# Two channel blocks of v in one load, with a newly planned instruction order, in an interleaved state-space kernel

## The chip, the cores and the metric

The kernel runs on one core of a Trainium2 chip. The metric is the device time of one execution in microseconds (us): the median of three runs. The core has five engines that run their own instruction streams and wait for each other through semaphores: TensorE (PE, matrix products, which land in eight PSUM banks), VectorE (DVE), ScalarE (ACT), GpSimd (POOL) and SyncE (SP). Transfers between the memory of the chip and the core's SBUF are started by an engine's queue, here nearly all by SP's, and are carried by 16 DMA engines.

## The reference

Four layers follow each other on a sequence of 2048 tokens with 640 channels, each added to its input: A, B, A, B, where the two A layers share their weights, and so do the two B layers.

```
x = A_x
x = x + A(layernorm(x))     # A: complex diagonal recurrence
x = x + B(layernorm(x))     # B: long convolution of k*v, gated
x = x + A(layernorm(x))
x = x + B(layernorm(x))

A(x): Lam_bar = exp(dt*Lam);  Bu = x @ B_bar.T
      h[t] = Lam_bar*h[t-1] + Bu[t]
      y = 2*Re(h @ Cmat.T) + x*Dskip
B(q): k_shift[t] = sum over l<4 of k[t-l]*shift_k[:,l]
      kv = k_shift * v
      y = causal convolution of kv with ssm_k (length 2048) + kv*ssm_D
      return q*y
```

In B only q is the layer's input; k and v are inputs of the kernel. So the long convolution y is the same in both B layers and is computed once.

## The kernel before

**Tiling.** The convolution goes in five passes, one for each block of 128 channels (yq0 to yq4), as a Fourier transform of 4096 points made of matrix products. The layers go in four chunks of 512 tokens (c0 to c3): A1c0 is the first A layer's chunk 0, B1c0 the first B layer's, A2 and B2 the second ones.

**Tasks.** The program is cut into some 900 tasks, each a few instructions with a name. The names that are needed here:

- `warm`: 18 products that warm TensorE up. `a_...`: the A layer's weights, as `a_b0` (products) with `a_b0e` (copies out of PSUM), and `a_ct` (products), `a_wc` (ScalarE) and `a_wm` (VectorE, line 493).
- `yt_...`: the tables of the transform; `yt_ph`, `yt_f2`, `yt_neg` run on VectorE, `yt_sin` on ScalarE, `yt_Ci` and `yt_Si` are DMA transposes (line 1047).
- `kv_kd`, `kv_k0`: a load of ssm_D and its cast on VectorE (line 1164).
- `kv_lk`, `kv_lv`: the load of one block of k (a DMA transpose, line 1209) and of v (line 1198). `kv_mm0:1` is the shift convolution of block 0, half 1, on TensorE; `kv_ev0:1` multiplies it by v on VectorE (line 1243). The two halves of a block are transposed by `yq0_vl` (line 1329).
- In a pass: `KA`, `KB` transform the filter, `VA`, `VB` the product kv, `pw` multiplies the two on VectorE (lines 1350 to 1354), `IB`, `tt` (DMA transpose), `IA` transform back, `st` stores the result. `yq1_IB:m3` is a group of products, `yq1_IB:e3` its copy out of PSUM (line 290 on ScalarE, 292 on VectorE).
- In an A chunk: `ln_bn`, `ln_sd`, `ln_post`, `id` normalise; `tu` transposes; `bq`, `bp` multiply by B; `eq`, `ev` copy out; `ri`, `sc`, `ro`, `hx` are the recurrence on VectorE (lines 803, 804, 820, 875); `cp` multiplies by C on TensorE (line 901), `xe` adds the result to x (line 911 on VectorE, 909 on ScalarE).
- In a B chunk: `ln_sq` and others normalise, `u`, `mm`, `m` gate and add (lines 959, 980, 982; 944 and 948 at the very end), `st` stores the output.

**Order.** No scheduler runs when the program is built: `ORDER` (line 59) is a written list of all task names, and each engine gets its instructions in that order. A letter after a name chooses the engine (`/a` ScalarE, `/d` VectorE, `/p` GpSimd). `PLACE` (line 144) gives each buffer its place in one SBUF arena (in units of 64 bytes) and each PSUM tile its first bank. Buffers share places, and an instruction waits until the last reader of what lay there before is done; so order, engines and places together set every wait. SP, too, works through its transfers in this order: one that waits holds up all behind it.

SP's transfers up to the first half of the convolution are, in this order: B_im, B_re, filter 0, k0, v0, x0, filter 1, k1, v1, `yq0_vl`, C_re, x2, C_im, filter 2, `yt_Ci`, k2, `yt_Si`, v2, x1, `yq1_vl`, k3, v3, `yq2_vl`, `yq0_tt`, x3, `A1c0_tu`, `yq3_vl`, k4, filter 3, v4, `yq0_st`. A load of v brings 2048 rows of 256 bytes (128 channels in bf16).

Of the kernel before, what the change touches and what calls it, by code (L numbers as in the profile page):

```python
# [17 lines left out]
P = 128  # L18
# [3 lines left out]
NJ = D // P  # L22
# [17 lines left out]
VN = 1  # L40
# [19 lines left out]
a_ldB1 a_ldB0 yt_io8 yt_ph8 kv_dsl kv_kd yq0_kl a_pl a_ti yt_h0 yt_io0 kv_pd2/p yt_f0 kv_lk0 kv_k0 yt_ph0 yt_f2 kv_d0  # L60
kv_lv0 warm kv_k1 a_b01:2 yt_sin8 xl0 yq1_kl kv_lk1 a_p0 kv_lv1 yt_sin0 yt_f3 a_b0e1:2/a a_p1 a_b00:4 a_b00:2 yt_neg8
kv_pd4/d kv_k2 yt_f4 kv_pd0/p a_p2 yq0_ka a_b0e0:4/a a_b01:3 yq0_KA:m0 a_b0e0:2/a a_p3 a_b00:3 a_b0e1:3/d yq0_KA:e0/d
kv_pd3/d kv_d1 kv_d2 a_p4a a_p4 kv_ds0 kv_ds1 a_dd yt_h1 kv_ds4 kv_ds3 kv_ds2 a_b00:1 a_b0e0:3/a a_b0e0:1/a a_b01:0
yt_neg0 a_b0e1:0/a a_b00:0 a_b0e0:0/a yq0_KA:m3 yq0_KA:e3/a yq0_KA:m2 kv_mm0:1 yq0_KA:e2/d kv_pd1/d a_ta yq0_KA:m1
a_b01:4 yq0_KA:e1/a kv_mm0:0 a_b0e1:4/a kv_ev0:1 a_t0 kv_ev0:0 yq0_vl a_ldC0 xl2 a_ldC1 a_p5a a_p5b yq0_KB:m0
yq0_KB:e0/a yq0_KB:m2 yq2_kl yt_Ci kv_lk2 yq0_KB:e2/a yt_Si a_p6 kv_lv2 yq1_ka a_f A1c0_ln_bn:1/d a_lamd/d yq1_KA:m1
yq1_KA:e1/a xl1 yq1_KA:m2 yq0_KB:m3 yq1_KA:m3 kv_mm1:0 yq1_KA:e3/a a_b01:1 yq1_KA:e2/a yq0_KB:e3/a kv_ev1:0 yt_h2
a_b0e1:1/a yt_h3/p a_t1 kv_mm1:1 kv_ev1:1 a_b11:3 yq0_VA:m2 a_b1e1:3/d yq0_VA:e2/d a_b11:0 a_b1e1:0/d a_b10:1
a_b1e0:1/d yq0_KB:m1 a_b11:1 a_b1e1:1/a yq0_KB:e1/d a_b11:4 yq0_VA:m1 yq0_VA:e1/a a_b1e1:4/d yq0_VA:m3 yq0_VA:m0
yq0_VA:e3/d yq1_KA:m0 yq0_VA:e0/a a_b10:4 a_t2 A1c0_ln_bn:2/d A1c0_ln_bn:3/d A1c0_ln_bn:0/d yq1_KA:e0/a a_b1e0:4/a  # L70
yq0_VB:m0 yq0_VB:e0/a a_ct1 yq0_VB:m3 a_wc01:0 a_wm01:0 yq0_VB:m2 yq0_VB:e3/a yq0_VB:e2/a a_wc01:1 A1c0_ln_sd a_b10:2
a_lm2 yq2_ka a_b1e0:2/d a_wm01:1 yq0_VB:m1 yt_nci yq1_KB:m1 yq0_VB:e1/a a_b11:2 yq1_KB:m2 yq1_KB:e1/a kv_mm2:0
a_b1e1:2/a yq1_KB:e2/a A1c0_ln_post yq0_pw:0 a_b10:3 a_b10:0 a_b1e0:3/a yq1_vl kv_mm2:1 a_b1e0:0/a kv_lk3 kv_lv3
A1c0_id:2/a A1c0_id:0/a yq1_KB:m3 yq1_KB:e3/a yq1_KB:m0 kv_ev2:1 yq1_KB:e0/a yq2_KA:m3 yq2_KA:e3/a yt_nsi kv_ev2:0
yq2_vl A1c2_ln_bn:1/d A1c2_ln_bn:3/d A1c2_ln_bn:2/d A1c1_ln_bn:2/d A1c1_ln_bn:3/d A1c2_ln_bn:0/d A1c0_id:1/a
A1c0_id:3/a A1c1_ln_bn:1/d yq0_IB:m0 yq2_KA:m0 yq0_IB:e0/a yq2_KA:e0/a yq0_IB:m1 yq0_IB:m3 yq0_IB:e1/a yq0_IB:e3/a
yq1_VA:m2 yq1_VA:m1 yq1_VA:e2/a yq0_IB:m2 A1c2_ln_sd yq1_VA:m3 yq0_IB:e2/a yq0_tt yq1_VA:m0 A1c1_ln_bn:0/d yq1_VA:e0/d
yq1_VA:e3/a yq1_VA:e1/a kv_mm3:1 a_ct4 A1c1_ln_sd yq1_VB:m1 a_wc04:0 kv_ev3:1 kv_mm3:0 A1c2_ln_post a_wm04:0
A1c1_ln_post yq1_VB:e1/a a_wc04:1 kv_ev3:0 yq1_VB:m0 A1c2_id:0/a a_wm04:1 yq1_VB:m3 a_ct0 A1c2_id:2/d A1c2_id:3/d
yq1_VB:e3/d A1c2_id:1/d xl3 A1c0_tu yq1_VB:e0/a a_wc00:0 yq1_VB:m2 yq0_IA:m1 yq1_VB:e2/a yq0_IA:m0 yq3_vl kv_lk4  # L80
yq3_kl kv_lv4 a_wm00:0 a_wc00:1 a_wm00:1 yq0_IA:e1/a yq0_IA:e0/a yq2_VA:m2 yq2_VA:e2/a yq1_pw:0 yq2_VA:m1 yq2_VA:e1/a
yq2_KA:m1 yq2_VA:m3 yq2_VA:e3/a yq2_KA:m2 a_ct2 yq2_KA:e2/a yq2_KA:e1/a a_wc02:0 yq2_VA:m0 yq2_KB:m0 yq2_VA:e0/a
yq2_KB:e0/a a_wm02:0 A1c1_id:1/d A1c1_id:0/d A1c3_ln_bn:0/d a_wc02:1 yq2_KB:m1 yq1_IB:m0 a_wm02:1 yq0_st
A1c3_ln_bn:3/d A1c3_ln_bn:1/d A1c3_ln_bn:2/d yq2_KB:e1/a yq1_IB:m3 yq1_IB:e0/a yq1_IB:e3/a a_ct3 a_wc03:0 a_wm03:0
yq1_IB:m1 yq1_IB:e1/a yq1_IB:m2 yq1_IB:e2/d a_wc03:1 a_wm03:1 yq3_ka yq2_KB:m2 A1c1_id:2/a yq2_KB:e2/a A1c3_ln_sd
yq1_tt kv_mm4:1 yq2_KB:m3 kv_ev4:1 A1c1_id:3/a yq2_KB:e3/a yq3_KA:m3 yq3_KA:m0 yq3_KA:e0/a yq3_KA:e3/d yq4_kl
yq2_VB:m0 yq2_VB:m3 yq2_VB:m2 yq2_VB:e0/d yq2_VB:e3/d yq3_KA:m2 A1c0_bq:2 A1c3_ln_post yq2_VB:e2/d yq3_KA:e2/a
kv_mm4:0 yq3_KA:m1 A1c0_eq:2/a yq2_VB:m1 A1c0_bp:2 yq3_KA:e1/a kv_ev4:0 A1c1_tu yq2_VB:e1/d yq2_pw:0 yq1_IA:m1
yq3_VA:m0 A1c0_ev:2/a yq3_VA:e0/a yq1_IA:e1/a A1c0_bq:1 A1c0_eq:1/a yq3_VA:m2 yq3_KB:m0 yq3_VA:m1 A1c0_bp:1 A1c2_tu
yq3_KB:e0/a yq3_VA:e2/a yq3_VA:e1/a yq3_VA:m3 yq3_KB:m3 yq3_VA:e3/d yq4_ka A1c3_id:1/d A1c3_id:3/d yq3_KB:e3/d  # L90
A1c3_id:0/d A1c0_ev:1/a yq2_IB:m2 yq3_KB:m2 yq2_IB:m0 yq2_IB:e2/a yq3_KB:e2/a yq3_VB:m3 yq2_IB:e0/d yq3_VB:e3/a
yq1_IA:m0 yq1_IA:e0/d A1c3_id:2/a yq3_VB:m0 yq3_VB:m2 yq3_VB:e2/d yq2_IB:m1 yq4_KA:m2 yq3_VB:e0/a a_rq yq3_KB:m1
yq3_KB:e1/a yq2_IB:m3 yq2_IB:e1/d yq2_IB:e3/a yq3_VB:m1 yq1_st A1c3_tu yq3_VB:e1/d yq3_pw:0 yq2_tt yq4_vl A1c0_bq:0
yq4_KA:e2/a A1c0_eq:0/a yq4_KA:m3 A1c1_bq:0 yq4_KA:m0 yq4_KA:e3/a yq4_KA:m1 A1c0_bp:0 yq4_KA:e0/a yq4_KA:e1/a
A1c2_bq:2 yq4_KB:m1 A1c0_ev:0/a A1c0_ri yq3_IB:m3 a_rq2 A1c0_sc A1c0_cy A1c0_ro A1c0_hx A1c1_eq:0/a yq4_KB:e1/a
A1c1_bq:2 yq2_IA:m0 A1c2_eq:2/a yq3_IB:e3/a A1c2_bp:2 yq2_IA:m1 yq2_IA:e0/a A1c2_ev:2/a A1c1_eq:2/a yq2_IA:e1/a
A1c1_xr A1c0_xr yq2_st A1c1_bq:1 yq4_KB:m2 A1c1_bp:2 A1c1_eq:1/a A1c1_bp:1 yq4_KB:e2/a A1c1_ev:2/a yq4_VA:m2 yq3_IB:m0
yq4_VA:e2/a A1c1_bp:0 yq3_IB:e0/a A1c1_ev:1/a yq4_KB:m3 A1c1_ev:0/a yq3_IB:m1 yq4_VA:m3 yq4_KB:m0 yq4_KB:e3/a
yq4_VA:e3/d yq4_KB:e0/d yq3_IB:e1/a A1c2_bq:0 A1c1_ri A1c1_sc A1c1_cy yq4_VA:m0 yq4_VA:m1 yq4_VA:e1/a A1c2_eq:0/a
A1c2_bq:1 yq3_IB:m2 yq4_VA:e0/a yq3_IB:e2/a A1c2_eq:1/a A1c2_bp:0 A1c2_ev:0/a yq4_VB:m3 yq4_VB:m2 A1c2_bp:1 yq4_VB:m0  # L100
yq4_VB:e2/a A1c2_ev:1/a yq4_VB:m1 yq4_VB:e3/a yq4_VB:e1/a A1c0_cp:1 A1c0_xe:1/a yq4_VB:e0/d yq4_pw:0 a_w10:2 yq3_tt
a_w10:1 a_w11:4 a_w1e0:2/a a_w11:0 A1c0_cp:3 a_w1e0:1/a a_w1e1:0/a a_w1e1:4/a a_w10:3 yq4_IB:m2 A1c0_xe:3/d A1c1_ro
A1c2_ri A1c2_sc a_w1e0:3/a yq4_IB:e2/a a_w10:0 a_w1e0:0/a a_w11:3 a_w1e1:3/a yq4_IB:m0 yq4_IB:e0/a a_w11:2 a_w1e1:2/a
yq4_IB:m1 yq4_IB:e1/a a_w10:4 yq4_IB:m3 a_w11:1 A1c1_cp:3 yq4_IB:e3/a a_w1e0:4/a a_w1e1:1/a yq3_IA:m0 yq3_IA:m1 yq4_tt
A1c0_cp:0 A1c1_xe:3/d A1c0_xe:0/d a_lamd2/a yq3_IA:e0/a yq3_IA:e1/a A1c3_bq:2 A1c3_eq:2/d A1c0_cp:2 A1c0_xe:2/d yq3_st
yq4_IA:m0 yq4_IA:m1 yq4_IA:e0/d yq4_IA:e1/a yq4_st A1c2_xr A1c3_bp:2 B1l0 A1c1_hx A1c1_cp:1 A1c2_cy A1c2_ro
B1c0_ln_sq:3 B1c0_ln_sq:1 B1c0_ln_sq:0 B1c0_ln_sq:2 B1c0_ln_sd B1c0_ln_post B1c0_u:3/a B1c0_u:1/a A1c3_e2:2/a
A1c1_cp:0 A1c1_xe:0/d A1c1_cp:2 B1c0_u:0/a A1c1_xe:1/d A1c1_xe:2/d B1c0_u:2/d B1c1_ln_sq:3 B1c1_ln_sq:2 B1c1_ln_sq:1
B1c1_ln_sq:0 A1c3_bq:0 B1c1_ln_sd A1c3_eq:0/a B1c0_mm A1c3_b4:2 A1c3_bq:1 A1c2_cp:1 B1c0_m:2 B1c0_m:0 B1c0_m:3
B1c0_m:1 A1c3_bp:0 B1c1_ln_post A1c3_eq:1/d A1c3_ev:2/d A2c0_ln_sq:1 A2c0_ln_sq:3 A2c0_ln_sq:0 A2c0_ln_sq:2 A2c0_ln_sd  # L110
B1l2 A1c3_xr B1l1 A1c2_hx B1c1_u:2/d A1c2_xe:1/d A1c3_bp:1 A1c2_cp:3 A2c0_ln_post A2c0_id:3/d A2c0_id:1/d A2c0_id:0/d
A2c0_id:2/a B1c1_u:0/a B1c1_u:3/d B1c1_u:1/d B1c1_mm B1c1_m:3 A1c3_e2:1/a B1c1_m:0 B1c1_m:1 B1c1_m:2 A1c2_xe:3/d
A1c3_b4:1 A1c3_e2:0/a A1c3_b4:0 A1c2_cp:2 A1c3_ev:1/a A1c3_ev:0/a a_tq/a A1c3_ri A2c0_tu A2c1_ln_sq:1 A2c1_ln_sq:3
A2c1_ln_sq:2 A2c1_ln_sq:0 A1c2_cp:0 A1c2_xe:2/d A1c2_xe:0/d A2c0_bq:0 A2c0_bq:2 A2c0_bq:1 A2c0_eq:0/a B1c2_ln_sq:0
A2c1_ln_sd A1c3_sc A1c3_ro A2c1_ln_post A2c1_id:0/d A1c3_hx:1 B1c2_ln_sq:2 B1c2_ln_sq:1 B1c2_ln_sq:3 B1c2_ln_sd
A2c0_eq:1/a A2c0_bp:0 B1c2_ln_post B1c2_u:3/d B1c2_u:0/d B1c2_u:1/d A2c0_eq:2/a A2c1_id:1/a A2c1_id:2/a B2l1 A1c3_h1:2
A1c3_h1:0 A1c3_eh:0/a A1c3_h1:1 A1c3_eh:1/a A1c3_eh:2/a B1c2_u:2/d B1c2_mm B1c2_m:0 B1c2_m:3 A2c0_bp:1 A2c0_bp:2
A2c1_id:3/a A2c0_ev:0/a A2c0_ev:1/a A2c0_ev:2/a A2c1_tu B1l3 A1c3_cp:3 A1c3_cp:2 A1c3_hx:0 B1c2_m:1 B1c2_m:2
# [1023 lines left out]
def kv_tasks(S, nc, wp, St, consts, B_k, B_v, B_shift_k, B_ssm_D):  # L1142
# [48 lines left out]
    for kb in range(NJ):  # L1191
        s_kT = S.slot(f"kT{kb}", 2 * (KPAD + L), lambda t: t)
        if kb % VN == 0:
            nv = min(VN, NJ - kb)
            s_vv = S.slot(f"v{kb}", 2 * L * nv, lambda t, nv=nv: t.rearrange("p (a n) -> p a n", n=nv * P))
# [4 lines left out]
        s_kv = S.slot(f"kv{kb}", 2 * L, lambda t: t)  # L1200
# [16 lines left out]
        for h in range(2):  # L1217
            s_pk = S.bank(f"pk{kb}{h}", 2)
# [341 lines left out]
```

## Time and profile before

| | |
|---|---|
| median of 3 runs | 339.01 us (338.83 to 339.64) |
| the profiled execution | 339.59 us, of which the profile's span is 337.4 us |
| granted TensorE clock, mean | 0.98 |
| TensorE busy (products) | 310.9 us, 92% of the span |
| VectorE busy | 313.1 us, 93% |
| ScalarE busy | 253.4 us, 75% |
| GpSimd busy | 20.4 us, 6% |
| DMA | 41.61 MB in 105097 packets; SP's queue 56.0% of 16 engines' span |
| loads of v | 5, of 512 KB each, 5.9 us from issue to landing (median) |

Three engines are above 70% of the span, so no single one sets the time throughout. The windows view gives the busy time of each engine in a stretch: an engine that is busy in all of it sets the pace there. A timeline line says when an instruction began and, in brackets, how long its engine stood idle before it and which instruction ended that. The time of an execution is 2.2 us longer than the profile's span.

### The profile page before, as it was taken

What the parts mean: (1) busy time and instruction counts of PE and PEld (TensorE: products, weight loads), DVE (VectorE), ACT (ScalarE), POOL (GpSimd) and SP (SyncE); (2) the same over time, 40 slices, a digit from 0 to 9 for tenths busy, and PEclk for the clock granted to TensorE, in tenths of its full rate; (3) what the DMA queues carried; (4) which work ended last, traced back from release to release, by engine and by line L of the source; (5) the groups of instructions that cost most, each with busy time, mean ns of one, the idle gap of its engine ahead of it and who ended that gap; (6) DMA issues with size and microseconds to landing.
All of it is one profiled execution on the core that took longest, in us unless ns stands there. A gap on an engine that the chain in (4) does not pass through costs nothing. (4 is left out here: it accounts for less than half of the span.)

```text
span 337.4 us, 8902 instructions
## 1 busy us (share of the span) xinstructions
PE 310.9 (92%) x3819; PEld 242.3 (72%) x3838; DVE 313.1 (93%) x477; ACT 253.4 (75%) x396; POOL 20.4 (6%) x51
## 2 busy tenths in 40 slices
PE   7678899868999999999998999999999999999991
PEld 3567688757888989887666678686685777775651
DVE  5999989989999799998998989999999999999996
ACT  5989999999967879665784687797885755482682
POOL 4496000000000000000000000000000000000000
PEclk9979999996999999999999999999999999999998
DMA  8999999899994683250645671404230260014014
GB/s 236 253 178 312 191 226 191 131 209 171 196 195 90 127 142 64 67 153 2 120 90 105 184 270 36 122 2 80 87 70 1 80 157 0 2 40 118 0 41 194
DMA packets 105097, 41.61 MB, mean 123 GB/s; under 512 B 97885, under 2 KB 100450, under 8 KB 105058
## 3 DMA queue, kind: packets, MB, share of 16 engines
q1 hardware_dynamic: 104912, 41.03, 56.0%
q8 instruction: 30, 0.49, 0.6%
q14 instruction: 9, 0.07, 0.1%
q10 hardware_dynamic: 146, 0.01, 0.0%
HBM read 19.02 MB, written 5.24 MB: 72 GB/s over the span
## 5 line engine op out<-in xcount | busy, mean ns | idle before, releaser
L290 ACT ACTIVATE arena<-banks 128x1024 bf16<-128x1024 f32 (+3 forms) x156 | 134.2, 910 | 43.7 <-PE banks L765 10.7
L901 PE MATMUL banks<-arena 128*128 128x128 bf16 (+1 forms) x782 | 98.5, 281 | 1.4 <-DVE arena L911 0.3
L901 PEld LDWEIGHTS <-arena 128*128 128x128 bf16 x800 | 59.7, 98 | 40.7 <-issue 2.1
L750 PE MATMUL banks<-arena 128*128 128x256 bf16 x400 | 46.5, 273 | 1.4 <-ACT arena L290 1.4
L765 PE MATMUL banks<-arena 128*128 128x256 bf16 x400 | 46.5, 273 | 0.0
L644 ACT ACTIVATE junk<-arena,sums 128x640 bf16<-128x640 f32 x48 | 39.6, 825 | 7.3 <-DVE arena L980 4.4
L750 PEld LDWEIGHTS <-arena 128*128 128x128 bf16 x400 | 38.4, 98 | 6.2 <-issue 1.6
L765 PEld LDWEIGHTS <-arena 128*128 128x128 bf16 x400 | 38.5, 98 | 4.4
L1294 PE MATMUL banks<-arena 128*128 128x256 bf16 x160 | 39.7, 286 | 1.4 <-ACT arena L290 0.9
L803 DVE TENSOR_TENSOR arena<-arena 128x5160 bf16<-128x5160 bf16 (+1 forms) x16 | 40.2, 2511 | 0.5
L696 ACT ACTIVATE arena<-arena,nmr,rstd 128x640 bf16<-128x640 f32 (+1 forms) x36 | 31.3, 915 | 12.0 <-DVE nmr L657 12.0
L292 DVE CAST arena<-banks 128x1024 bf16<-128x1024 f32 (+3 forms) x34 | 35.9, 1085 | 4.1 <-PE banks L1296 2.6
L820 DVE TENSOR_TENSOR_SCAN arena<-arena 128x1290 bf16<-128x1290 f32 (+1 forms) x16 | 39.3, 2500 | 0.2
L1295 PE MATMUL banks<-arena 128*128 128x128 bf16 x160 | 36.3, 227 | 0.0
L1296 PE MATMUL banks<-arena 128*128 128x128 bf16 x160 | 36.2, 227 | 0.0
L911 DVE SCALAR_TENSOR_TENSOR arena<-banks,arena 128x640 f32<-128x640 f32 x27 | 21.6, 819 | 3.2 <-PE banks L901 3.1
L1376 PE MATMUL banks<-arena 128*128 128x128 bf16 (+1 forms) x288 | 24.2, 237 | 0.4 <-DVE arena L493 0.4
L1376 PEld LDWEIGHTS <-arena 128*128 128x128 bf16 x288 | 20.7, 98 | 2.0 <-issue 0.5
L804 DVE TENSOR_TENSOR arena<-arena 128x2580 bf16<-128x2580 bf16 (+1 forms) x16 | 21.4, 1337 | 0.5
L1296 PEld LDWEIGHTS <-arena 128*128 128x128 bf16 x160 | 16.3, 102 | 2.5
L1295 PEld LDWEIGHTS <-arena 128*128 128x128 bf16 x160 | 16.3, 102 | 2.0 <-issue 1.9
L1294 PEld LDWEIGHTS <-arena 128*128 128x128 bf16 x160 | 16.3, 102 | 1.2 <-issue 0.2
(205 smaller groups left out, 406.6 us busy)
## 6 DMA issues: line engine op xcount, KB each, us to landing
arena<-in_A_x_dram SPq DMA_DIRECT2D x8, 640.0 KB, 7.3
arena<-ysd SPq DMA_DIRECT2D x8, 640.0 KB, 4.5
arena<-in_B_ssm_k_dram SPq DMA_DIRECT2D x5, 512.0 KB, 5.3
arena<-in_B_v_dram SPq DMA_DIRECT2D x5, 512.0 KB, 5.9
ysd<-arena SPq DMA_DIRECT2D x5, 512.0 KB, 4.0
out_dram<-arena SPq DMA_DIRECT2D x8, 320.0 KB, 2.2
arena<-in_A_B_im_dram SPq DMA_DIRECT2D x1, 800.0 KB, 4.9
arena<-in_A_B_re_dram SPq DMA_DIRECT2D x1, 800.0 KB, 6.8
```

The costliest lines, as they stand in the source:

```text
L290: nc.scalar.activation(out, in_, ACT.Copy)
L292: nc.vector.tensor_copy(out, in_)
L644: nc.scalar.activation(small.junk, src(q), ACT.Square, bias=sums()[:, i:i + 1], scale=-float(D), accum_out=st["ssq"][:, i:i + 1])
L750: nc.tensor.matmul(pb[:, jj, c2, :], lhsT=bt0[:, c2, k, j * P:(j + 1) * P], rhs=uT[:, 2:4, k, :], start=(c2 == k == 0), stop=(c2 == 1 and ...
L765: nc.tensor.matmul(pb[:, jj, c2, :], lhsT=bt1[:, c2, j, k, :], rhs=uT[:, 0:2, k, :], start=False, stop=(c2 == 1 and k == NJ - 1), skip_gro ...
L803: nc.vector.tensor_tensor(tt, gs[:, :, None].to_broadcast([P, 2, 2, n]), by_pairs(tab.get().rearrange("p i j b -> p (i j b)"), n), ALU.mult)
L820: nc.vector.tensor_tensor_scan(gv, rt, gv, 0.0, ALU.mult, ALU.add)
L901: nc.tensor.matmul(pc[:, o0:o1], lhsT=lh, rhs=rh, start=(n == 0), stop=(n == len(ops) - 1))
L1294: nc.tensor.matmul(ps[:, g], lhsT=T["Cf"].get()[:, q, :], rhs=A[:, 2 * q:2 * q + 2, :], start=True, stop=False, skip_group_check=True)
L1295: nc.tensor.matmul(ps[:, g, 0, :], lhsT=T["Sf"].get()[:, q, :], rhs=aim, start=False, stop=False, skip_group_check=True)
L1296: nc.tensor.matmul(ps[:, g, 1, :], lhsT=T["NSf"].get()[:, q, :], rhs=are, start=False, stop=True, skip_group_check=True)
L1376: nc.tensor.matmul(ps[:, bi + b0:bi + b1, :], lhsT=T[tb].get()[:, q, :], rhs=rh, start=(n == 0), stop=(n == len(ops) - 1), skip_group_chec ...
```

## The change

Blocks 0 and 1 of v are loaded by one transfer, and so are blocks 2 and 3; block 4 stays alone. A row of a double load is 512 bytes. There are three loads of v (1 MB, 1 MB, 512 KB) in place of five, and the tasks `kv_lv1` and `kv_lv3` are gone. `kv_ev0` and `kv_ev1` now read the two halves of one buffer, as do `kv_ev2` and `kv_ev3`.

```diff
-VN = 1
+VG = {0: 2, 2: 2, 4: 1}
...
-        if kb % VN == 0:
-            nv = min(VN, NJ - kb)
+        if kb in VG:
+            v0, nv = kb, VG[kb]
             s_vv = S.slot(f"v{kb}", 2 * L * nv, lambda t, nv=nv: t.rearrange("p (a n) -> p a n", n=nv * P))
...
-                v = s_vv.get()[:, 8 * h:8 * (h + 1), P * (kb % VN):P * (kb % VN + 1)].rearrange("p a (q e) -> p q a e", e=4)
+                v = s_vv.get()[:, 8 * h:8 * (h + 1), P * (kb - v0):P * (kb - v0 + 1)].rearrange("p a (q e) -> p q a e", e=4)
```

The rest of the diff replaces the whole of `ORDER` and of `PLACE`. The same 894 other tasks stand in a new order, most buffers and banks have a new place, and 62 tasks have another engine: 29 move from VectorE to ScalarE or GpSimd, 33 from ScalarE or GpSimd to VectorE. The start of the list shows the manner:

```diff
-a_ldB1 a_ldB0 yt_io8 yt_ph8 kv_dsl kv_kd yq0_kl a_pl a_ti yt_h0 yt_io0 kv_pd2/p yt_f0 kv_lk0 kv_k0 yt_ph0 yt_f2 kv_d0
-kv_lv0 warm kv_k1 a_b01:2 yt_sin8 xl0 yq1_kl kv_lk1 a_p0 kv_lv1 yt_sin0 yt_f3 a_b0e1:2/a a_p1 a_b00:4 a_b00:2 yt_neg8
...
+warm kv_dsl kv_kd a_pl a_ldB1 kv_pd3/d kv_pd4/d yt_io0 yt_f0 yt_ph0 yt_sin0 yt_f2 kv_pd0/d yt_h0 yt_io8 kv_pd1/p a_ti
+a_b01:2 a_ldB0 yt_ph8 kv_pd2/p yt_h1 kv_k0 kv_d0 yt_neg0 a_p0 kv_k1 yt_f3 yt_f4 kv_k2 yt_sin8 a_p1 a_p2 a_b0e1:2/a
...
```

Further places that the prediction speaks of:

- SP's transfers now are: B_im, B_re, filter 0, k0, v0 with v1, x0, filter 1, k1, x1, `yq0_vl`, C_im, C_re, `yt_Ci`, k2, `yt_Si`, x2, v2 with v3, filter 2, `yq1_vl`, k3, `yq2_vl`, `yq0_tt`, x3, filter 3, `A1c0_tu`, `yq0_st`, k4, v4, `yq3_vl`.
- After `yq1_pw` VectorE did `a_wm02:0`, two `A1c1_id`, one `ln_bn`, `a_wm02:1`; now it does `a_wm02:0`, one `ln_bn`, `a_wm02:1`. The bank of `yq1_IB:m3` lies under that of `a_ct2`, which `a_wm02:1` reads last, in both kernels.
- In the bank places, `yq3_VB:m2` now lies where `yq3_KB:e2` reads, which has moved from ScalarE to VectorE (it lay elsewhere before), and `yq2_KB:m3` now lies over a bank of `a_ct3`, which `a_wm03:1` on VectorE reads last. `kv_mm4:1` lies in the bank that `yq1_IB:e2` on VectorE sets free, in both kernels.
- After `A1c1_cp:3` TensorE's order was `yq3_IA`, `A1c0_cp:0`, `A1c3_bq:2`, `A1c0_cp:2`; now `A1c0_cp:2` stands ahead of `A1c3_bq:2`. On ScalarE one of the two copies `yq3_IA:e` now stands ahead of `a_lamd2` (15 instructions of line 431), where both stood behind it. The copy `A1c3_eq:2`, which stood ahead of `A1c0_xe:2` on VectorE, is now ScalarE's.
- The last tasks of the list, from `A2c3_cp:1` over `A2c3_xe:1` on ScalarE to `B2c31_m:1` and the last store, form the same chain in both.

## Prediction

> **What bounds the kernel now.** I read the engines' totals first, then the slices, then the windows, and the timeline where the windows left a question.
>
> ```profile
> PE 310.9 (92%) x3819; PEld 242.3 (72%) x3838; DVE 313.1 (93%) x477; ACT 253.4 (75%) x396; POOL 20.4 (6%) x51
> PE   7678899868999999999998999999999999999991
> DVE  5999989989999799998998989999999999999996
> ACT  5989999999967879665784687797885755482682
> PEclk9979999996999999999999999999999999999998
> ```
>
> The totals say TensorE and VectorE together. The slices (8.4 us each) show more: ScalarE stands at 9 up to slice 10 and TensorE at 6 to 8 just there. So the first quarter differs from the rest, which the windows put in numbers (start:end, span, busy time of PE, PEld, DVE, ACT, POOL, clock, DMA share, GB/s):
>
> ```profile
> 0.00:10.00 10.00, 6.83 (x25) 2.85 (x25) 5.78 (x33) 6.25 (x9) 3.64 (x17) 1.00 0.91 231
> 10.00:20.00 10.00, 6.94 (x198) 5.68 (x198) 9.86 (x29) 9.46 (x16) 6.56 (x13) 1.00 1.17 225
> 30.00:40.00 10.00, 8.01 (x129) 6.88 (x129) 9.80 (x21) 9.94 (x14) 0.91 (x3) 1.00 1.10 263
> 70.00:80.00 10.00, 6.32 (x102) 5.17 (x102) 9.07 (x9) 9.73 (x11) 0.00 (x0) 0.75 1.24 201
> 90.00:158.00 68.00, 67.95 (x901) 59.41 (x900) 61.85 (x54) 50.42 (x59) 0.00 (x0) 1.00 0.54 110
> 158.00:334.00 176.00, 169.54 (x1515) 122.02 (x1531) 170.03 (x239) 120.54 (x226) 0.00 (x0) 1.00 0.32 84
> ```
>
> Three regimes. From 10 to about 88 us VectorE and ScalarE are both full, and TensorE waits for their copies. From 90 to 158 TensorE has no gap (67.95 of 68.00): it alone sets the time. From 158 VectorE loses 6.0 us of 176 and TensorE 6.5: each waits for the other. DMA is at its limit (share over 1) only in the first quarter, where the changed loads lie.
>
> The waits that the new order can touch, and the starts that I sum from:
>
> ```profile
> 5.96 0.17 DVE L1164 CAST arena<-arena 80x8 f32<-80x8 bf16 x1 [2.83 <-DMA arena<-in_B_ssm_D_dram]
> 9.98 0.58 SPq L1198 DMA_DIRECT2D arena<-in_B_v_dram  x1
> 17.95 1.20 DVE L1243 TENSOR_TENSOR arena<-banks,arena 128x1024 bf16<-128x1024 f32 x1
> 46.27 2.29 DVE L1350 TENSOR_TENSOR arena<-arena 128x4096 bf16<-128x4096 bf16 x1 [0.54 <-ACT arena L290]
> 72.92 2.28 DVE L1350 TENSOR_TENSOR arena<-arena 128x4096 bf16<-128x4096 bf16 x1
> 184.84 0.82 DVE L911 SCALAR_TENSOR_TENSOR arena<-banks,arena 128x640 f32<-128x640 f32 x1 [1.68 <-PE banks L901]
> 195.78 0.83 DVE L911 SCALAR_TENSOR_TENSOR arena<-banks,arena 128x640 f32<-128x640 f32 x1 [1.15 <-PE banks L901]
> 333.31 0.89 DVE L948 SCALAR_TENSOR_TENSOR arena<-arena,rstd 128x640 bf16<-128x640 bf16 x1
> ```
>
> **The sums' base.** Each profile is one execution: 339.59 us, of it 337.4 in the span and 2.2 around it; it is 0.58 above the median of 339.01. I sum on 339.59 and carry the difference to the median.
>
> **1. The start.** VectorE stood 2.83 us for ssm_D before `kv_k0`. By the new order `yt_ph0`, `yt_f2` and `yt_ph8` stand ahead of it, together 3.6 us more (start-to-start spacings of their rows: 1.05, 2.2, 1.0, less two small casts). These were work behind the wait, so the wait goes if their inputs, small POOL and DMA results, are there; I keep 2.0 of 2.83, since TensorE's warm-up ends only at 8.2 to 8.4 us. Bounds 0 and −2.8.
>
> **2. The loads of v.** v0 went out at 9.98 and took 4.9 us to land. The double one carries 0.5 MB more, 1.4 us at the 360 to 380 GB/s that the rows of 1280 bytes reached at the start, 1.8 us at some 290 in full stretches of 256-byte rows: it lands at 9.98 + 4.9 + 1.4…1.8 = 16.3…16.7, issue unmoved. `kv_ev0:1` began at 17.95; with 2.0 us gained it could begin at 16.0. So 0.3…0.7 us of the gain is lost: 0.5 taken, bounds 0 and 1.5 (nothing gained on the rate, landing at 17.5). With x1 (640 KB) ahead of `yq0_vl` in place of v1 (512 KB), later transfers on SP's queue move by 0.1 MB, 0.4 us; `yt_Ci` comes earlier, behind 1.6 MB instead of 2.7 MB. v2 with v3 should land near 45…48 us, and their first use is near 50: zero, hidden by that slack; at most +2 if the queue is late.
>
> [...]
>
> **3. The saturated stretch, up to 88 us.** I added, along each written order, the spacing of every VectorE and ScalarE instruction ahead of a landmark. Ahead of `yq0_pw` (46.27): VectorE 40.0 before, 40.1 after; ScalarE 42.3, then 39.3. So it keeps the start's gain: −2.0 + 0.5 = −1.5, it begins at some 44.8. Ahead of `yq1_pw` (72.92): VectorE 65.1, then 67.2, +2.1; ScalarE 66.4, then 66.9. VectorE's waits between the two were 0.9 us and more (0.86 stood just before the second), of which I give back 0.9: −1.5 + 2.1 − 0.9 = −0.3. After `yq1_pw` two normalisations of 0.36 (spacing of line 698) come out from ahead of `a_wm02:1`, on which `yq1_IB:m3` and so TensorE wait: −0.7. At `kv_mm4:1` (88.17) the sums are 81.4 and 81.6 for VectorE, 80.3 and 78.8 for ScalarE, 65.6 twice for TensorE: equal or less. **TensorE enters its bound stretch 1.0 us earlier**; bounds −2.0 (the whole start kept, without the wait for v) and +1.0 (nothing kept, VectorE's 2.1 paid in half).
>
> The clock lies in here too: 0.75 in 70 to 80 us. In 75 to 82 us each group of three transform products started 0.43 us after the last one, in 88 to 93 us only 0.22. If the new order avoids or repeats such a spell, ScalarE's waits say what is at stake: 0.36 us was lost to TensorE there. I take 0, bounds −0.4 and +1.9 (one more spell like that of 20 to 24 us, clock 0.58). [...]
>
> **4. The TensorE-bound stretch, 88 to 158 us.** Its products and their order hardly change: 0. The cover is that VectorE and ScalarE stay ahead; see the third rival.
>
> **5. The rest, 158 to 334 us.** Over the program 33 tasks come to VectorE and 29 leave. With the mean rows (1219 ns for a transform copy, 816 for one of 640, 439 or 608 for a normalisation, 1025 and 704, 912 to 927 on ScalarE) this is VectorE +1.4, ScalarE −3.3 us; behind `yq4_pw`, VectorE has 173.6 before and 175.0 after: all +1.4 falls into this stretch, where VectorE is 97% full. Against it: `A1c0_xe:2` waited 1.68 us for `A1c0_cp:2`, which now stands ahead of `A1c3_bq:2` (products of some 1.1 us), and one copy of `yq3_IA` no longer waits behind the 4.5 us of `a_lamd2`. I take −1.2 off the 1.68 and −0.3 off the 1.15: +1.4 − 1.5 = −0.1. Bounds −2.8 + 1.4 = −1.4 and +1.4.
>
> **6. The end** (`A2c3_cp:1`, copy, normalisation, line 948 at 333.31, store) is the same chain: 0.
>
> **Sum:** −1.0 + 0 − 0.1 + 0 = −1.1; 339.59 − 1.1 = 338.5 in the profiled frame, **337.9** against the median.
>
> **Rivals.**
> *B, the gain stays whole.* The start keeps 2.0 to TensorE's stretch, both later waits vanish, and of VectorE's +1.4 a third lies in the gaps that are left (6.0 us). −2.0 − 2.8 + 0.9 = −3.9: **335.1**. For: the sums at `kv_mm4:1` are no greater. Against: the +2.1 ahead of `yq1_pw`.
> *C, slower: VectorE holds TensorE's banks.* `yq3_VB:m2` now waits for `yq3_KB:e2`, which moved to VectorE, and `yq2_KB:m3` for `a_wm03:1`; between 76 and 112 us VectorE's queue has more in front of them. TensorE's stretch without gaps then gets one of up to 2.3 us (a copy and one line-1350 product, 1.2 + 1.1 left of it), and nothing behind it can win that back; with +1.4 of VectorE behind it, 339.0 + 2.3 + 1.4 = **342.7**. It decides from the point where VectorE is not 1.5 us ahead of TensorE there. For: ScalarE, free in 158 to 334, gives work away to a full VectorE. Against: VectorE idles 6 of the 68 us, so it seems to be ahead.
> *D, the loads were hidden anyway* and the order gives as much as it takes: **339.0**; for it speaks that VectorE, and not DMA, ends the waits after 6 us.
>
> **From cases to numbers.** A change below 0.3%, 1.02 us, cannot be told from none here. Forecast 0.42: −1.1 lies at that bound; its own range is 336.6 to 339.3, so 0.23 faster, 0.16 same, 0.03 slower. B 0.21, all faster. C 0.33, all slower. D 0.04, same. Together 0.44, 0.20, 0.36. The range reaches past B by 1.6 (the rest of the start's wait 0.8, the clock's 0.4, half of the 0.9) and past C by 1.3 (two thirds of one more clock spell's 1.9): 333.5 to 344.0.
>
> **What would show it.** VectorE without a wait of 2 us in the first 8; the first multiply of `yq0_pw` near 44.8 and that of `yq1_pw` near 72.6; three loads of v, the first landing by 16.7; `kv_mm4:1` near 87.2; from there to 158 TensorE without a gap; a wait under 0.6 before `A1c0_xe:2`; VectorE busy 314.5, ScalarE 250. It is wrong if `kv_ev0:1` waits over 1.5 us for v, if TensorE shows gaps from 90 to 158, or if the second half differs from before by over 1.5 us.

## The result, and the profile after

The changed kernel takes 341.57 us (median of 6 runs, 341.1 to 342.17) where the kernel before takes 339.13 in the same comparison: a ratio of 1.0073, 95% interval 1.0056 to 1.0090. It is slower by 0.7%. Executions of one kernel differ among themselves (of 132 of the kernel before in all sessions, 14 took 340.2 to 341.4 us and the others 338.3 to 340.1), and a profile shows one execution. The changed kernel's profiled execution has a span of 340.2 us, 2.8 more than before.

The totals and three rows of slices of the changed kernel's page:

```profile
PE 313.7 (92%) x3838; PEld 243.2 (71%) x3838; DVE 313.8 (92%) x479; ACT 249.9 (73%) x396; POOL 18.8 (6%) x51
PE   7757789968999999999999999999999999999991
DVE  7968999999989599996999999999999999999995
ACT  5969999989768867668588668699566475453772
```

VectorE is 0.7 us busier (+1.4 was summed) and ScalarE 3.5 us less (−3.3 was). But VectorE has a 6 in its third slice and ScalarE a 6 too, where both had 8 or 9. The windows view of the changed kernel (columns as before) says how much that is:

```profile
10.00:20.00 10.00, 6.16 (x186) 5.06 (x184) 8.30 (x20) 9.95 (x19) 7.16 (x16) 1.00 1.20 274
20.00:30.00 10.00, 7.60 (x178) 6.42 (x179) 7.18 (x12) 6.64 (x11) 4.42 (x11) 0.83 1.04 190
90.00:158.00 68.00, 67.46 (x948) 59.05 (x946) 61.98 (x58) 49.88 (x59) 0.00 (x0) 1.00 0.62 106
158.00:334.00 176.00, 173.73 (x1565) 124.29 (x1563) 169.12 (x240) 119.53 (x225) 0.00 (x0) 1.00 0.33 85
```

From 10 to 30 us VectorE, which should be full, is idle for 4.5 us, and ScalarE from 20 to 30 for 3.4. The later stretches look as before: TensorE is busy for 67.46 of 68 us from 90 to 158, and is busier than before behind it. So the loss is made early. The timeline of the changed kernel names it:

```profile
16.61 1.22 DVE L1241 TENSOR_TENSOR arena<-banks,arena 128x1024 bf16<-128x1024 f32 x1
21.42 0.37 PE L1225 MATMUL banks<-arena 64*128 64x64 bf16 x7 [3.41 <-issue]
21.90 1.22 DVE L1241 TENSOR_TENSOR arena<-banks,arena 128x1024 bf16<-128x1024 f32 x1 [3.33 <-PE banks L1225]
23.65 1.02 ACT L288 ACTIVATE arena<-banks 128x1024 bf16<-128x1024 f32 x1 [2.96 <-PE banks L1294]
48.03 2.29 DVE L1348 TENSOR_TENSOR arena<-arena 128x4096 bf16<-128x4096 bf16 x1
75.95 2.28 DVE L1348 TENSOR_TENSOR arena<-arena 128x4096 bf16<-128x4096 bf16 x1
197.84 0.82 DVE L909 SCALAR_TENSOR_TENSOR arena<-banks,arena 128x640 f32<-128x640 f32 x1 [0.79 <-PE banks L899]
```

`kv_ev0:1` does start earlier, at 16.61 instead of 17.95. Then TensorE stops in the middle of `kv_mm0:0`, 57 products in, for 3.41 us, and what ends the wait is "issue": nothing that an engine or a load did. VectorE and ScalarE run dry behind it. The first multiply (`yq0_pw`) comes at 48.03 (46.27 before), the second at 75.95 (72.92). The same stop stands in the timeline of the kernel before, a third as long:

```profile
20.82 0.37 PE L1227 MATMUL banks<-arena 64*128 64x64 bf16 x7 [1.02 <-issue]
```

TensorE's distance from the kernel before, weight load by weight load (the n-th against the n-th), gives the account: −1.8 us just ahead of the stop, +0.7 behind it, +1.9 at 30 us, +2.7 at 88, +3.1 at 170, +2.1 at 185, +2.5 at its last product.

**What the stop is.** The page of DMA queues has, in both kernels, the same line for instructions (queue, packets, MB, share of 16 engines):

```profile
q8 instruction: 30, 0.49, 0.6%
```

30 packets of 16 KB, against 3819 to 3838 products and as many weight loads on TensorE: one packet for some 255 of them. In the trace's packet records the first of these begins at 18.28 us and lasts 1.25 in the kernel before, and TensorE goes on 1.28 us after its end; in the changed kernel it begins at 18.71 and lasts 1.31, and TensorE goes on 1.40 after its end. So the first theory: TensorE ran out of instructions, and its next block travelled on the same 16 DMA engines as v, x and the filters. Windows of half a us of the two kernels show the company it had, before (18.0 to 18.5) and after (18.5 to 19.0); the queue of the loads alone took 164% and 131% of the engines' time:

```profile
q1 hardware_dynamic: 353, 0.09, 163.9%
q8 instruction: 1, 0.02, 15.7%
```

```profile
q1 hardware_dynamic: 442, 0.11, 130.6%
q8 instruction: 1, 0.02, 16.3%
```

The rival: the new order and engines cost the time in the saturated stretch, and the stop only stands in front of other waits. The clock is no rival between these two kernels: it is 0.83 from 20 to 30 us in both, one spell of half clock of 3.4 us each.

### The profile page after: what moved, and what is told of

It is laid out like the page before. It is cut to its first block, busy times and chain, and to the rows that moved or that the text cites. A ratio compares the mean times of both kernels' runs of the same rounds, so it can differ in the third digit from the quotient of the medians.

```text
span 340.2 us, 8926 instructions
## 1 busy us (share of the span) xinstructions
PE 313.7 (92%) x3838; PEld 243.2 (71%) x3838; DVE 313.8 (92%) x479; ACT 249.9 (73%) x396; POOL 18.8 (6%) x51
## 5 line engine op out<-in xcount | busy, mean ns | idle before, releaser
L288 ACT ACTIVATE arena<-banks 128x1024 bf16<-128x1024 f32 (+3 forms) x158 | 135.8, 906 | 48.5 <-PE banks L748 18.2
L899 PE MATMUL banks<-arena 128*128 128x128 bf16 (+1 forms) x800 | 100.2, 283 | 0.9 <-DVE arena L802 0.6
L290 DVE CAST arena<-banks 128x1024 bf16<-128x1024 f32 (+2 forms) x32 | 35.1, 1113 | 4.7 <-PE banks L1294 2.8
L694 ACT ACTIVATE arena<-arena,nmr,rstd 128x640 bf16<-128x640 f32 (+1 forms) x29 | 25.7, 913 | 11.0 <-DVE nmr L655 10.2
L1374 PE MATMUL banks<-arena 128*128 128x128 bf16 (+1 forms) x288 | 25.0, 242 | 0.0
L1293 PEld LDWEIGHTS <-arena 128*128 128x128 bf16 x160 | 16.3, 102 | 3.3 <-issue 3.0
L1294 PEld LDWEIGHTS <-arena 128*128 128x128 bf16 x160 | 16.3, 102 | 2.7
L1292 PEld LDWEIGHTS <-arena 128*128 128x128 bf16 x160 | 16.3, 102 | 1.3 <-issue 0.2
```

What stands on the lines that cost most here:

```text
L288: nc.scalar.activation(out, in_, ACT.Copy)
L290: nc.vector.tensor_copy(out, in_)
L899: nc.tensor.matmul(pc[:, o0:o1], lhsT=lh, rhs=rh, start=(n == 0), stop=(n == len(ops) - 1))
L1292: nc.tensor.matmul(ps[:, g], lhsT=T["Cf"].get()[:, q, :], rhs=A[:, 2 * q:2 * q + 2, :], start=True, stop=False, skip_group_check=True)
L1293: nc.tensor.matmul(ps[:, g, 0, :], lhsT=T["Sf"].get()[:, q, :], rhs=aim, start=False, stop=False, skip_group_check=True)
L1294: nc.tensor.matmul(ps[:, g, 1, :], lhsT=T["NSf"].get()[:, q, :], rhs=are, start=False, stop=True, skip_group_check=True)
```

## The experiments

Eighteen kernels ran, e1 to e18, each timed against the kernel before in the same session. Behind a label stand the median, the ratio to the kernel before and its 95% interval.

### Moving the ends of the instruction blocks (e1, e4, e5, e12)

If blocks have a fixed number of instructions, more instructions at the very start move every block end to an earlier piece of the work. The warm-up is the place: nobody reads its products.

```diff
-        for i in range(18):
+        for i in range(14):
             nc.tensor.matmul(s_warm.get().rearrange("p (a n) -> p a n", n=P), lhsT=consts["ident_bf"][:], rhs=consts["ident_bf"][:, None, :].to_broadcast([P, 4, P]), start=True, stop=True)
+        for i in range(60):
+            nc.tensor.matmul(s_warm.get()[:, 0:64], lhsT=consts["ident_bf"][:], rhs=consts["ident_bf"][:, 0:64], start=True, stop=True)
```

The changed kernel with it:

> The changed kernel; of the 18 warm-up products of 512 columns 14 stay, and 60 of 64 columns follow them in the same bank, so that TensorE's instruction stream is 112 rows longer ahead of all real work and every block of 256 instructions is asked for earlier. Theory 1 (instruction fetch): TensorE's third block is asked for when TensorE passes row 182 and arrives behind the loads of v, x and filter 1; it is 3.4 us late, and that wait costs the start's gain and starves ScalarE and VectorE. Then the request falls near 10 us, the wait inside kv_mm0:0 is below 0.5 us, TensorE is still 1 to 2 us ahead of the kernel before at 19 us, and the time falls by 2 to 4 us, to 337.5 to 339.5. Theory 2 (the new order and engines in the full stretch to 50 us cost the time, the wait only stands in front of other waits): the wait goes, but the time stays within 0.7 us of 341.6.

Measured: 339.34 us, ratio 1.0006 (0.9992 to 1.0019), 2.2 us below the changed kernel. The stop in `kv_mm0:0` is gone. It did not vanish altogether; a stop of its kind stands elsewhere, in the timeline of e1 and, for the kernel before with the same warm-up (e4), here:

```profile
29.13 0.21 PE L1225 MATMUL banks<-arena 64*128 64x64 bf16 x1 [2.29 <-issue]
```

```profile
29.67 0.19 PE L1227 MATMUL banks<-arena 64*128 64x64 bf16 x1 [1.42 <-issue]
```

Counting TensorE's recorded instructions ahead of each stop gives 449 (223 weight loads, 222 products, 4 others) in the kernel before, the changed one, e2, e3, e6, e8, e9, e13 and e17, and 961 (478, 477, 6) in e1, e4, e5, e7, e10, e11 and e14. The difference is 512, two blocks of 256, whatever work stands there. Two smaller waits for "issue" come later, 0.51 us in e3 after 1473 instructions and 0.30 us in e5 after 2241: four and seven times 256 behind 449. All eighteen waits ended 1.23 to 1.48 us after the end of a 16-KB packet of queue q8. Nothing but the instruction stream has that count, so the first theory's mechanism is shown.

> The kernel before with the same longer warm-up as in e1 (14 products of 512 columns and 60 of 64). Theory 1: TensorE's wait of 1.0 us inside kv_mm0:0 goes and the time falls by 0.3 to 1.2 us, to 337.9 to 338.8. Theory 2: within 0.3 us of 339.1.

e4: 339.47 us, 1.0006 (0.9988 to 1.0024). The first wait went and a later one came: no gain, against expectation.

A shift of 72 instructions (40 small products in place of 60) lies better for the third block:

> The changed kernel with a warm-up of 14 products of 512 columns and 40 of 64: 72 rows longer than its own, where e1 was 112 longer. By the rows of e1, TensorE then needs its blocks at rows that it reaches 5.9, 4.7 and 7.2 us after it asked for them (e1: 7.0, 4.9 and 3.0, and it waited 2.3 us at the third). Theory 1 (the waits are instruction fetches at every 256th row): the wait of e1 at its row 694 goes, 0.5 to 1.5 us in all are left at the first two, and the time falls below e1's 339.3, to 337.3 to 339.0. Theory 2 (the order and engines of the changed kernel cost what e1 lost again between 27 and 50 us): the time stays at 339.3 within 0.5 or above it.

e5: 339.29, 1.0014 (0.9995 to 1.0033). Its waits for instructions are 0.81 and 0.3 us, but it is no faster than e1, which had one of 2.29: this is the time that the second theory expected. So a part of the forecast gain is missing without the long stop too. Some of that stands at the start, where `kv_ev0:1` now waits for the double load (0.43 us in e1), in the timeline of e5:

```profile
17.55 1.22 DVE L1241 TENSOR_TENSOR arena<-banks,arena 128x1024 bf16<-128x1024 f32 x1 [1.28 <-DMA arena<-in_B_v_dram]
```

The windows of e1 say why a stop can be free (26 to 30 us of e1, then 18 to 24 us of the changed kernel):

```profile
26.00:30.00 4.00, 1.71 (x65) 1.35 (x58) 3.90 (x10) 3.97 (x5) 0.00 (x0) 0.83 0.99 282
```

```profile
18.00:24.00 6.00, 2.59 (x24) 2.14 (x23) 2.67 (x5) 3.02 (x5) 5.14 (x16) 0.76 1.22 209
```

At 29 us VectorE (3.90 of 4.00) and ScalarE (3.97) have work queued and hardly notice; at 18 to 24 they have none (2.67 and 3.02 of 6.00), and they set the pace. The first multiply (`yq0_pw`) comes at 45.74 in e1 and at 45.80 in e5, whose stop is 1.5 us shorter.

> The kernel before with the warm-up of e5 (72 rows more; e4 had 112 more, lost its first fetch wait of 1.0 us and got one of 1.4 us at 29 us). Theory 1: neither wait is above 0.5 us and the time falls by 0.4 to 1.2 us. If VectorE and ScalarE set the time to 75 us whatever TensorE waits, the time stays within 0.3 us.

e12: 338.68, 0.9991 (0.9976 to 1.0006): no stop, and no difference in time that can be measured. That does not say that the stop of 1.0 us was free: weight load by weight load, e12's TensorE is 1.0 us ahead of the kernel before's profile from 36 to 220 us, and 0.3 at its end. But that profile is of an execution of 339.59 us, 0.6 above the median, and the stop is not always that long (0.49 us in e17, which is the same kernel up to there).

### The load alone, and what of it counts (e2, e6, e15)

> The kernel before in its own order, engines and places, with one change: blocks 0 and 1 of v come in one load of 512-byte rows, issued where v0 was; its buffer lies in a free place, and v1's load is gone. Theory 1: 0.5 MB more lies ahead of the third instruction block, whose wait in the DMA engines grows from 2.9 towards 4.3 us; TensorE's wait inside kv_mm0:0 grows from 1.0 to 2 us or more; the time rises by 0.5 to 2 us, to 339.6 to 341.1. Theory 2: the load is harmless, the wait stays at 1.0 and the time within 0.4 us of 339.1.

```diff
-VN = 1
+VG = {0: 2, 2: 1, 3: 1, 4: 1}
-... kv_lv0 ... kv_lv1 ...
+... kv_lv0 ...
-    "v0": 289
+    "v0": 2739
```

e2: 341.09, 1.0061 (1.0038 to 1.0084). The stop grew as the first theory expected:

```profile
22.32 0.37 PE L1227 MATMUL banks<-arena 64*128 64x64 bf16 x7 [2.67 <-issue]
```

TensorE is 1.5 us later just behind it, 1.9 at 26 us, 2.3 at 36 us, and 2.3 at the end: nothing later gives it back. Half clock, granted for 3.4 us around 20 to 24 us in the kernel before, lasted 6.8 us here, which may be a part of it. Is it the 512-byte rows, or the half megabyte ahead of the instruction packet? e6 has two single loads, one behind the other:

> The kernel before; only the load of block 1 of v is issued straight behind that of block 0, as a load of its own in 256-byte rows. The same bytes lie ahead of the third instruction block as in e2, without the double rows. Theory 1a (it is the bytes ahead of the fetch that count): the wait inside kv_mm0:0 is 2 us or more and the time 340.5 to 342, as in e2 (341.1) or worse. Theory 1b (it is the single transfer or its 512-byte rows that hold the fetch up): the wait stays near 1.0 to 1.5 and the time within 0.6 us of 339.1.

```diff
-... kv_lv0 warm ... a_p0 kv_lv1 ...
+... kv_lv0 kv_lv1 warm ... a_p0 ...
```

e6: 341.53, 1.0082 (1.0055 to 1.0110), with a stop of 2.93 us at the same instruction (in a profile of 343.02 us). So the bytes ahead count; whether wide rows are any better cannot be told (the intervals of e2 and e6 overlap).

> e2 (the kernel before with the double load, 341.1) with the warm-up of e12 (72 rows more). If the load costs only through the late instruction block: no fetch wait over 1 us, and 338.6 to 339.4, the 2 us being gone. If it costs by itself (block 0 waits for block 1's bytes, more traffic ahead of x and k): 340.3 to 341.2.

e15: 338.54, 0.9993 (0.9982 to 1.0005). The double load's 2 us are gone, with the same load at the same place: in this order it cost through the late instruction block and what follows from that. No stop is left. With it went the half clock at 20 us (e15 has a spell of 3.4 us at 14 us instead), so the price of a stop holds that too; the two were not parted.

### The order alone (e3, e9, e10, e11, e7)

> The changed kernel with its order, engines and places; only the first double load of v is cut in two: block 0 (256-byte rows) at its place, block 1 into the other half of the same buffer behind the second load of k. Theory 1: 0.5 MB less lies ahead of the third instruction block, its wait falls from 4.3 to about 3 us, TensorE's from 3.4 to about 2.2, and the time falls by 1 to 2 us, to 339.6 to 340.6. Theory 2: the time stays within 0.5 us of 341.6.

```diff
-                nc.sync.dma_start(out=s_vv.get(), in_=B_v[0][:, kb * P:(kb + nv) * P].rearrange("(a i) d -> i a d", i=P))
+                n1 = 1 if kb == 0 else nv
+                nc.sync.dma_start(out=s_vv.get()[:, :, 0:n1 * P], in_=B_v[0][:, kb * P:(kb + n1) * P].rearrange("(a i) d -> i a d", i=P))
...
+        elif kb == 1:
+
+            def e_lv(_, s_vv=s_vv):
+                nc.sync.dma_start(out=s_vv.get()[:, :, P:2 * P], in_=B_v[0][:, P:2 * P].rearrange("(a i) d -> i a d", i=P))
...
-kv_lk1
+kv_lk1 kv_lv1
```

e3: 340.87, 1.0059 (1.0037 to 1.0082). The packet began a us earlier (17.70) and the stop fell to 2.00 us, about as expected; the time fell by less.

> The changed kernel's order, engines and places with five single loads of v again: block 1 behind the second load of k, block 3 behind the fourth, each into the other half of the double buffer. Beside e2 (the double load alone, 341.1 against 339.2) this is the order alone. Theory 1 (the load is what costs): 338.5 to 340.0; TensorE's fetch wait stays at some 2 us, as in e3, since TensorE reaches its 512th row early. Theory 2 (the order costs): 340.5 or above.

(block 3 in the same way, behind `kv_lk3`.) e9: 341.07, 1.0066 (1.0050 to 1.0082), stop 2.75 us: the expectation of the first theory failed. The order alone is as slow as the load alone. It is the same stop: TensorE arrives 2.0 us earlier than in the kernel before, its block only 0.4 (the packet ends at 19.13 instead of 19.54).

> e9 with the warm-up of e5 (72 rows more). Theory 1: no v late and fetch waits of at most 1.6 us in all; the first multiply of yq0_pw at 44.5 to 45.2, as in e7, and no wait for v at 50 us, which cost e7 2.1 us: 337.0 to 338.5, and no runs near 342 as e7 had. Theory 2: 339 or above, the lead being lost by the second multiply.

e10: 339.51, 1.0026 (1.0013 to 1.0038). The first multiply comes at 45.10 (46.27 before), the second at 72.93 (72.92): the start's gain is there, and is spent by then, as the second theory had it. A stop of 1.64 us is left at 30 us, and the profile is of an execution of 338.73 us, 0.8 below the median.

> e10 with the load of block 2 of v issued ahead of that of x2 (640 KB) and not behind it. If v is still what the faster start runs into at 50 us, 0.5 to 1 us below e10; if v has slack again, the same as e10 within 0.4 us, or later by what waits for x2.

e11: 340.12, 1.0031 (1.0014 to 1.0047): nothing gained. In e10's profile, too, VectorE does not wait for v there.

> e3 (block 1 of v behind the second load of k) with the warm-up of e5. Theory 1: both the bytes ahead of the fetches and their phase are mended, no fetch wait over 0.7 us is left, and the time is the lowest of the changed kernel's kin: 336.8 to 338.5. Theory 2: 339.3 or above, since the time is lost in the order between 27 and 75 us.

e7: 340.36, 1.0059 (1.0031 to 1.0088), its runs between 339.0 and 343.6. Its first multiply came at 44.48, the earliest of all, and then the second double load was late, which its timeline shows:

```profile
51.94 1.23 DVE L1247 TENSOR_TENSOR arena<-banks,arena 128x1024 bf16<-128x1024 f32 x1 [2.12 <-DMA arena<-in_B_v_dram]
```

The load and the order in a table, ratio to the kernel before:

| | own warm-up | 72 instructions more |
|---|---|---|
| kernel before | 1 | 0.9991 (e12) |
| double load alone (first pair) | 1.0061 (e2) | 0.9993 (e15) |
| new order alone | 1.0066 (e9) | 1.0026 (e10) |
| both | 1.0073 (the changed kernel) | 1.0014 (e5) |

Load and order cost 0.6% each and 0.7% together: one stop, which either of them makes long enough to starve the other engines. With the block ends elsewhere the load costs nothing that can be measured, and the order, alone or with the load, 0.1 to 0.3% (e5's interval holds 1). Stops at 30 us are left in e10 (1.64 us) and e5 (0.81), so what the order costs with no stop at all was not measured.

### Between the two multiplies (e8, e13, e14)

The start's gain is spent between `yq0_pw` and `yq1_pw`, where VectorE has more to do. The windows of that stretch in the kernel before, the changed one, and e8:

```profile
46.27:72.92 26.65, 23.06 (x546) 20.70 (x545) 24.76 (x44) 25.10 (x32) 0.00 (x0) 1.00 1.04 186
```

```profile
48.03:75.95 27.92, 24.39 (x564) 21.66 (x563) 26.79 (x44) 25.40 (x35) 0.00 (x0) 1.00 1.02 172
```

```profile
48.12:77.88 29.76, 24.60 (x564) 21.77 (x563) 23.45 (x42) 27.81 (x39) 0.00 (x0) 1.00 0.97 160
```

> The changed kernel; the three copies yq2_KA:e3, yq0_IB:e1 and yq0_IA:e1, which it moved to VectorE between the first two multiplies yq0_pw and yq1_pw, go back to ScalarE. By the prediction's sum VectorE's extra work there costs 1.2 us net. If that holds, the stretch from the first to the second multiply shrinks from 27.9 to about 26.6 us and the time by 0.5 to 1.3 us, to 340.3 to 341.1; if ScalarE was as full there, both stay within 0.3 us.

```diff
-yq2_KA:e3/d ... yq0_IB:e1/d ... yq0_IA:e1/d
+yq2_KA:e3/a ... yq0_IB:e1/a ... yq0_IA:e1/a
```

e8: 343.75, 1.0138 (1.0109 to 1.0166). VectorE is 3.3 us freer and the stretch 1.8 us longer: ScalarE, at 27.81, now has more to do.

> The changed kernel; between the first two multiplies the exchange of engines is taken back: the copies yq2_KA:e3, yq0_IB:e1, yq0_IA:e1 to ScalarE (as in e8, which rose to 343.8) and the statistics A1c1_ln_bn:3 from ScalarE to VectorE. VectorE has 2.4 us less ahead of yq1_pw than in the changed kernel, ScalarE 0.8 more. If VectorE's extra work makes that stretch long: from the first to the second multiply 26.7 to 27.3 us instead of 27.9, and 340.6 to 341.2. If ScalarE is what is full there: 28.2 or more, and 341.6 or above.

e13: 343.99, 1.0151 (1.0128 to 1.0173), stretch 29.75 us. Here each of the two engines has less to do in it than VectorE had in the changed kernel (26.79), and it is longer all the same (windows of e13, then the last operation ahead of the second multiply in the timeline of e8; e13 has the same wait):

```profile
48.64:78.39 29.75, 24.61 (x564) 21.76 (x563) 24.40 (x44) 26.22 (x34) 0.00 (x0) 1.00 0.98 154
```

```profile
77.07 0.88 DVE L491 SCALAR_TENSOR_TENSOR arena<-banks,s_F,arena 128x640 bf16<-128x640 f32 x1 [2.18 <-ACT arena L487]
```

VectorE's `a_wm` waits 2.18 us for ScalarE's `a_wc`, ahead of which one more copy stands; in the changed kernel it did not wait there.

> e10 (order alone, longer warm-up, 339.5) with the exchange of e13. VectorE's theory: second multiply at 71.8 to 72.4 us, 338.3 to 339.1. ScalarE's theory: at 73.2 or later, 339.5 or above.

e14: 340.92, 1.0067 (1.0041 to 1.0092). The expectation for VectorE's theory failed three times: given this order, giving these copies back to ScalarE costs more than it frees. That does not refute what the theory says of the changed kernel, because e8 and e13 brought a new wait. From before to after, VectorE's work in the stretch grew by 2.03 us (24.76 to 26.79) and its idle time fell by 0.76, which makes the 1.27 by which the stretch grew; ScalarE's work grew by 0.30. That VectorE's extra work is the cause is argued from this sum; no run tried it by itself.

### The second half's gain (e17, e16, e18)

In the changed kernel TensorE wins back 1.0 us at 185 us. This piece of the order, alone:

> The kernel before with that piece of the new order alone. By the sum: the wait of 1.68 us ahead of A1c0_xe:2 falls below 0.5, TensorE is 1.0 us earlier at 185 us, and the time falls by 0.6 to 1.2 us. Rival: it is given back later, and the time stays within 0.3 us of the kernel before.

```diff
-A1c0_xe:0/d a_lamd2/a yq3_IA:e0/a yq3_IA:e1/a A1c3_bq:2 A1c3_eq:2/d A1c0_cp:2 A1c0_xe:2/d yq3_st ... yq4_IA:e1/a
+A1c0_xe:0/d yq3_IA:e1/a a_lamd2/a yq3_IA:e0/a A1c0_cp:2 A1c3_bq:2 A1c0_xe:2/d yq3_st ... yq4_IA:e1/a A1c3_eq:2/a
```

e17: 339.63, 1.0033 (1.0014 to 1.0052), slower. The wait of 1.68 us went and two came, as its timeline shows:

```profile
185.44 1.25 PE L765 MATMUL banks<-arena 128*128 128x256 bf16 x10 [1.60 <-ACT arena L290]
192.72 0.82 DVE L911 SCALAR_TENSOR_TENSOR arena<-banks,arena 128x640 f32<-128x640 f32 x1 [1.75 <-PE banks L901]
```

`A1c3_eq:2`, put behind `yq4_IA:e1` on ScalarE, came late, and `A1c3_bp:2` on TensorE waited for its bank.

> e15 (the kernel before with the double load and the longer warm-up, 338.5 beside 338.6) with one piece of the new order: yq3_IA:e1 ahead of a_lamd2 on ScalarE, A1c0_cp:2 ahead of A1c3_bq:2 on TensorE, and A1c3_eq:2 on ScalarE behind them. By the sum: A1c0_xe:2 waits under 0.5 us instead of 1.7, the lead of e15 stays and grows by 1.0 us at 185 us, and the time is 337.2 to 338.0, below both kernels. Rival: the stretch to 334 us, where VectorE is 97% full, gives it back, and the time stays within 0.4 us of 338.5.

e16: 339.76, 1.0032 (1.0020 to 1.0043), with the same two waits. With the copy left on VectorE, behind `A1c0_xe:2`:

> e16 with A1c3_eq:2 on VectorE, straight behind A1c0_xe:2. No wait of 1.6 us ahead of A1c3_bp:2 on TensorE, the 1.0 us gained at 185 us stays, and the time is 337.2 to 338.0, below the kernel before (338.6) by 0.6 us or more. Rival: the wait comes back in another place within the next 20 us, and the time stays within 0.4 us of e15's 338.5.

```diff
-... A1c3_bq:2 A1c0_xe:2/d yq3_st ... yq4_IA:e1/a A1c3_eq:2/a
+... A1c3_bq:2 A1c0_xe:2/d A1c3_eq:2/d yq3_st ... yq4_IA:e1/a
```

e18: 337.71, 0.9952 (0.9930 to 0.9973) (the medians alone give 0.9965). It is faster than both kernels: the old order and engines, the first double load, the block ends moved, and this one exchange. TensorE is 1.0 us earlier at 185 us than at 170 and keeps it to the end.

## Why the prediction was wrong

The forecast was 337.9, 0.3% faster; 341.57 lies in the range, on the side of the third rival (C, slower), but that rival's mechanism is not what happened: that the range held it was luck. Of the miss, 3.2 us lie ahead of the first multiply, which came at 48.03 where 44.8 was summed.

**1, the start.** The order of it held: VectorE no longer waits for ssm_D, and `kv_ev0:1` began at 16.61, 1.3 us earlier than before.

**2, the loads of v: the step that failed.** What it summed came true: the first double load landed at 16.52 (16.3 to 16.7 forecast). Block 0 waited for the double load in e1 and e5 (0.43 and 1.28 us), and not in the changed kernel. But the step said of the bytes moved forward that later transfers "on SP's queue move by 0.1 MB, 0.4 us". It counted one queue's transfers only. TensorE's instruction blocks, on another queue, are carried by the same 16 DMA engines (30 packets, 0.49 MB, 0.6% of their span), and of them no term speaks; the new order, which brings TensorE to its block end 1.8 us earlier, was summed as gain alone. Measured in their place: a stop of 3.41 instead of 1.02 us, and 2.5 us of TensorE's time between its rows at 19 and 24 us (from −1.8 to +0.7). The windows that the prediction showed had the DMA share at 1.17 from 10 to 20 us, and the timeline of before had the stop itself; neither was asked what instructions cost. The bound of +2 "if the queue is late" was put on the second double load. That one landed at 50.35 and not at 45 to 48, but its first use was at 53.30, so its 0 held; in e7, which was earlier, it did cost 2.12.

**3, the saturated stretch.** Without the stop the first multiply was expected at 44.8. It came at 44.48 in e7 and 45.10 in e10, but those have single loads at the start; with the double load it came at 45.74 in e1 and 45.80 in e5, where VectorE waits 0.43 and 1.28 us for v and then 1.72 and 0.82 for a filter (in e10 not for v, and 0.75 for the filter). So the stop in `kv_mm0:0` accounts for some 2.2 of the 3.2 us; 1.0 is left, over the 0.5 that the sum gave to v, and for the filter it had no term. From the first to the second multiply +1.2 was summed (2.1 of work, 0.9 of waits given back) and +1.27 measured (2.03 and 0.76). The −0.7 behind `yq1_pw` was there: TensorE's distance falls from +3.3 to +2.7. The half-speed clock spell at 75 to 86 us lasted 6.8 us in both kernels, so its 0 was right.

**4, TensorE's stretch.** 0 forecast, +0.4 measured (+2.7 at 88 us, +3.1 at 170). TensorE was busy for 67.46 of 68 us, so the third rival, gaps of up to 2.3 us for banks held by VectorE, fell. What is left of it is one wait, at `kv_mm4:1`, whose bank a copy on VectorE sets free (timeline of the changed kernel):

```profile
90.84 1.11 PE L1225 MATMUL banks<-arena 64*128 64x64 bf16 x64 [0.54 <-DVE arena L290]
```

**5, the rest.** −0.1 forecast; −0.3 measured (+3.1 at 170 us, +2.8 at the end of the span). No wait is left ahead of `A1c0_xe:2`, the 1.15 became 0.79, TensorE gained 1.0 at 185 us and gave half of it back.

## What to carry to other kernels

TensorE's instructions are loads too (here 30 packets of 16 KB, one for some 255 recorded instructions): where the DMA engines are full (a share of 1.17 and 1.20 from 10 to 20 us in these two kernels), add a term for them, and look for "issue" among its waits before moving bytes forward or work earlier. Such a stop costs only what it starves: in e1 2.29 us were nearly free, where VectorE and ScalarE had queues; in the changed kernel 3.41 cost 2.5, where they had none. And a few small products at the start are a cheap way to move the block ends.

## What the runs showed of the hardware that was not expected

TensorE's stops came after 449 or 961 recorded instructions in sixteen profiles, two smaller ones (0.51 and 0.30 us) at later multiples of 256, no other wait of its products for "issue" was above 0.2 us, and all eighteen ended 1.23 to 1.48 us after a 16-KB packet did. The longest was 3.71 us (e8). They vary: e17, which is the kernel before in its first 40 us, stopped for 0.49 us where that one's profile has 1.02. When a block is asked for is in no record; when its packet begins is. Where the DMA engines are less busy (share 0.33 from 158 to 334 us in the changed kernel), the last eleven packets of that kernel, from 182.12 us on, begin with 5055 to 7582 of TensorE's instructions recorded, 232 to 272 apart: 258 to 291 ahead of their block, if it is counted by 256 from 449. At the first stop, 256 ahead is 193, which TensorE passed at 15.50 us in the kernel before and at 14.51 in the changed one; the packets began at 18.28 and 18.71. So by estimate the first packet stood 2.8 us in the kernel before and 4.2 in the changed one before it began.
